# A Shen attention plus RWKV channel mix kernel: ranks of the planner passed back from the matmuls, mix-weight rows loaded by DMA, weight loads held by a wait

## The chip, the cores, the metric

The kernel runs on one core of one Trainium2 chip. The metric is the device time of one execution in microseconds (us), as a median over runs. The profile describes one of these executions; its span runs from the first to the last instruction, and the device time is about 1.8 us longer than the span. Engine names: PE is TensorE (matmuls), DVE is VectorE, ACT is ScalarE, POOL is GpSimd, SP is SyncE, which here issues loads and stores.

## The reference

Linear attention with both softmaxes, then a channel mix over its output. Shapes: q, k, v are 8 batches x 8 heads x 576 positions x 64; `w_k` is 512x1024, `w_v` 1024x512, `w_r` 512x512; everything arrives and leaves in fp32.

```python
q_s = softmax(q, axis=-1); k_s = softmax(k, axis=2)          # written out in the original
kv  = einsum('bhsd,bhse->bhde', k_s, v)
x   = einsum('bhsd,bhde->bhse', q_s, kv)                     # then (B, S, H*D)

x_prev = x shifted by one position, zero first
xk = mu_k * x + (1.0 - mu_k) * x_prev
xr = mu_r * x + (1.0 - mu_r) * x_prev
k  = np.maximum(xk @ w_k, 0.0)
v  = k * k @ w_v
r  = 1.0 / (1.0 + np.exp(-(xr @ w_r)))
return r * v
```

## The kernel before

The program is laid out by a planner written in Python. Each operation is added with its engine, how long it occupies the engine (`occ`), when its result is there (`lat`), a rank (`key`), the operations it depends on, and the buffers (`Slot`) that it takes and gives back. A list scheduler then fixes the order in which each engine's instructions are written. On the chip every engine works through its own list in that order, and semaphores make it wait where data or a buffer is not ready (in the run `g_held` below, ACT stands still for 3.22 us for a load, though the copy that comes after it in the list is ready).

```python
    def order(self):
        ...
                for op in ops:
                    if any(d.end is None for d in op.deps): continue
                    t = max([now] + [d.end + HOP for d in op.deps])
                    ...                                   # and until its buffers are free
                    rank = (max(t, now + 0.03), op.key)   # what starts first; ties by key
                    if ready is None or rank < ready[0]:
                        ready = (rank, t, op)
```

The keys of this kernel are written by hand (batch number times 200, and so on).

The work comes in two parts. *Attention* runs per batch and pair of heads (16 times): exponentials and casts on ACT, sums, scaling and mixing on DVE, and transposes and small matmuls on PE. The *main part* runs in ten units of 512 or 256 positions: the k product (line 593), ReLU on ACT (578), square on DVE (582), the r product (624), tanh on ACT (629), the v product (634), gating on DVE (640), store.

For batch 0 the mix with the shifted sequence is folded into the small matmuls of attention, which needs `mu` and `1 - mu` laid out as block masks. These rows are built by small fp32 matmuls:

```python
    def emit_mu_rows(m):
        for s in range(2):
            for ct in range(CT):
                for u in range(2):
                    to = mu_rows(m, s)[:, 128 * ct + 64 * u:128 * ct + 64 * u + 64]
                    nc.tensor.matmul(to, lhsT=pick[:, 4 * m + ct, u, :],          # line 305
                                     rhs=mu_sb[:, 64 * u:64 * u + 64], start=True,
                                     stop=(s == 0), skip_group_check=True)
                    if s == 1:
                        nc.tensor.matmul(to, lhsT=flip[:, u, :], rhs=ones[:],      # line 309
                                         start=False, stop=True, skip_group_check=True)
```

The loads of the weights and of batches 1 to 7 go out on POOL and are made to depend on one load of batch 0, `gate = [first[GATE]]` with `GATE = 7`: the second half of v of batch 0's first group. In the planner that orders their issue; nothing on the chip waits for the landing.

The softmax here doesn't subtract the row's maximum and nothing guards it: scores larger than these inputs give would overflow.

## Time and profile before

| | before |
|---|---|
| device time | 251.0 us (250.11 to 251.21) |
| span of the profiled run | 249.3 us |
| first k matmul of the main part | 38.9 us |
| last matmul ends | 244.4 us |

The page of the kernel before. The first line is busy time with the share of the span and the number of instructions; the rows below cut the span into 40 slices of 6.2 us, and each digit is the busy share in tenths. PEclk is the granted TensorE clock, also in tenths.

```profile
PE 220.9 (89%) x1377; PEld 120.0 (48%) x1377; DVE 164.7 (66%) x371; ACT 150.1 (60%) x228; POOL 39.2 (16%) x64
...
PE   0899889999478999989989998899999999999992
...
DVE  4920153588997998898999999998944233252331
...
PEclk9999999999959999999999999999999999999999
```

TensorE looks full from the second slice on. The chain of waits of the same kernel, which follows the work that ended last back through what released it, says what this early work is. Columns: start, duration, what.

```profile
2.11 5.05 DMA mu_sb<-in_moe_mu_r_dram
...
7.53 3.51 PE bank_c L305 x16
...
18.94 3.60 PE bank_d L305 x16
...
29.40 0.60 ACT mu_mask L316
...
32.20 1.12 PE bank_b L419 x9
...
38.89 0.86 PE bank_c L593 x4
```

From 7.5 to 29.4 us the chain is almost all small fp32 matmuls of lines 305 and 309. The first matmul of line 593, the k product, comes at 38.89. Up to there TensorE is busy, but not with the main part.

Two windows of the kernel before, the weakest later ones. Columns: the window and its length, then busy us (and instruction count) of PE, weight loads, DVE, ACT and POOL, then granted clock, DMA share, GB/s.

```profile
60.00:70.00 10.00, 5.56 (x76) 3.55 (x75) 9.84 (x23) 9.97 (x12) 5.54 (x8) 0.94 1.03 402
70.00:80.00 10.00, 9.14 (x62) 4.20 (x59) 8.58 (x19) 7.15 (x11) 2.24 (x4) 0.71 1.02 389
```

At 60 to 70 us TensorE waits while DVE and ACT are full; the clock then falls to 0.71 on average.

### The profile page before, as it was taken

How to read it: one execution, taken by the hardware profiler on the slowest of the kernel's cores; microseconds unless marked ns; L12 is line 12 of the kernel's file. 1: busy time of each engine (PE TensorE's matmuls, PEld its weight loads, DVE VectorE, ACT ScalarE, POOL GpSimd, SP SyncE). 2: the span in 40 equal slices, each digit the busy share in tenths (PEclk: the TensorE clock that was granted, in tenths of full speed). 3: DMA queues.
4: the chain of work that ended last, by engine and by line, in shares of the span. 5: the costliest groups of instructions: out<-in, count | busy, mean ns of one | idle time of the engine just before them, and what ended most of it. 6: DMA issues, size and time to landing. Idle time of an engine off the chain costs nothing.

```text
span 249.3 us, 3772 instructions
## 1 busy us (share of the span) xinstructions
PE 220.9 (89%) x1377; PEld 120.0 (48%) x1377; DVE 164.7 (66%) x371; ACT 150.1 (60%) x228; POOL 39.2 (16%) x64
## 2 busy tenths in 40 slices
PE   0899889999478999989989998899999999999992
PEld 0899854345234444344444456444444444444550
DVE  4920153588997998898999999998944233252331
ACT  4410255699968988998689885566235144244150
POOL 7323460043531133312000000000000000000000
PEclk9999999999959999999999999999999999999999
DMA  6999999059999679976510132120240330431413
GB/s 237 274 260 206 393 392 362 9 110 363 412 393 393 192 230 325 339 238 175 144 45 0 42 84 46 41 47 0 51 111 10 84 85 0 101 70 24 103 45 84
DMA packets 16402, 40.62 MB, mean 163 GB/s; under 512 B 2296, under 2 KB 4864, under 8 KB 16384
## 3 DMA queue, kind: packets, MB, share of 16 engines
q0 software_dynamic: 8896, 27.40, 34.8%
q1 hardware_dynamic: 7200, 12.39, 18.5%
q10 hardware_dynamic: 288, 0.59, 0.7%
q8 instruction: 11, 0.18, 0.3%
q14 instruction: 7, 0.06, 0.1%
HBM read 33.56 MB, written 9.44 MB: 172 GB/s over the span
## 4 chain that ended last, share of the span: by engine, by line
PE 63%; DVE 16%; ACT 12%; issue 4%; DMA 2%; POOL 0%; DVEq 0%; ACTq 0%; POOLq 0%
PE bank_c L593 11%; PE bank_c L634 10%; PE bank_d L634 9%; PE bank_d L593 9%; PE bank_d L624 6%; PE bank_c L624 4%; PE bank_a L309 3%; PE bank_a L305 3%; DVE qs_a L397 2%; DMA mu_sb<-in_moe_mu_r_dram 2%; PE bank_b L419 2%; ACT rel_b L578 2%; DVE ot_c L640 2%; PE bank_d L305 1%; PE bank_c L305 1%
## 5 line engine op out<-in xcount | busy, mean ns | idle before, releaser
L593 PEld LDWEIGHTS <-wk_bf 128*128 128x128 bf16 x320 | 30.6, 99 | 36.2 <-issue 9.0
L593 PE MATMUL bank_c<-xk,wk_bf 128*128 128x512 bf16 (+1 forms) x176 | 39.2, 357 | 0.7 <-ACT rel_b L578 0.3
L593 PE MATMUL bank_d<-xk,wk_bf 128*128 128x512 bf16 (+1 forms) x144 | 34.7, 372 | 3.0 <-DVE ot_a L640 0.7
L624 PEld LDWEIGHTS <-xr 128*128 128x128 bf16 x144 | 13.9, 97 | 18.6 <-issue 2.9
L624 PE MATMUL bank_d<-wr_bf,xr 128*128 128x512 bf16 x84 | 21.5, 378 | 0.9 <-ACT rel_c L578 0.6
L634 PEld LDWEIGHTS <-k_a 128*128 128x128 bf16 x144 | 13.5, 98 | 16.8 <-issue 1.8
L634 PEld LDWEIGHTS <-k_b 128*128 128x128 bf16 x144 | 13.6, 97 | 16.0 <-issue 1.2
L634 PE MATMUL bank_d<-wv_bf,k_a 128*128 128x512 bf16 x72 | 18.3, 379 | 0.9 <-ACT th_b L629 0.6
L634 PE MATMUL bank_d<-wv_bf,k_b 128*128 128x512 bf16 x72 | 18.5, 379 | 0.7 <-ACT th_a L629 0.6
L634 PE MATMUL bank_c<-wv_bf,k_b 128*128 128x512 bf16 x72 | 18.0, 379 | 0.2
L634 PE MATMUL bank_c<-wv_bf,k_a 128*128 128x512 bf16 x72 | 18.0, 379 | 0.0
L629 ACT ACTIVATE th_a<-bank_d 128x512 f32<-128x512 f32 x15 | 9.0, 602 | 12.8 <-PE bank_d L624 8.2
L624 PE MATMUL bank_c<-wr_bf,xr 128*128 128x512 bf16 x60 | 15.4, 379 | 0.3 <-ACT rel_c L578 0.3
L578 ACT ACTIVATE rel_b<-bank_c 128x512 bf16<-128x512 f32 (+1 forms) x16 | 8.9, 557 | 8.3 <-PE bank_c L593 8.3
L578 ACT ACTIVATE rel_a<-bank_c 128x512 bf16<-128x512 f32 (+1 forms) x16 | 8.5, 532 | 6.9 <-PE bank_c L593 6.4
L578 ACT ACTIVATE rel_c<-bank_d 128x512 bf16<-128x512 f32 (+1 forms) x14 | 7.6, 540 | 7.4 <-PE bank_d L593 4.2
L582 DVE TENSOR_TENSOR k_a<-rel_b 128x512 bf16<-128x512 bf16 (+1 forms) x14 | 5.7, 404 | 7.3 <-ACT rel_b L578 6.9
L316 ACT ACTIVATE mu_mask<-bank_a 128x512 f32<-128x512 f32 x2 | 1.2, 602 | 15.3 <-PE bank_a L309 15.3
L582 DVE TENSOR_TENSOR k_a<-rel_a 128x512 bf16<-128x512 bf16 (+1 forms) x13 | 5.1, 393 | 8.0 <-ACT rel_a L578 7.8
L629 ACT ACTIVATE th_b<-bank_c 128x512 f32<-128x512 f32 x12 | 7.2, 601 | 4.9 <-PE bank_c L624 2.0
L305 PE MATMUL bank_a<-mu_sb,pick 8*128 8x64 f32 x32 | 10.1, 416 | 0.0
L309 PE MATMUL bank_a<-ones,flip 1*128 1x64 f32 x32 | 10.1, 416 | 0.0
(214 smaller groups left out, 436.7 us busy)
## 6 DMA issues: line engine op xcount, KB each, us to landing
out_dram<-ot_a SPq DMA_DIRECT2D x24, 128.0 KB, 2.4
out_dram<-ot_b SPq DMA_DIRECT2D x24, 128.0 KB, 2.4
out_dram<-ot_c SPq DMA_DIRECT2D x24, 128.0 KB, 2.4
raw_a<-in_q_dram POOLq DMA_DIRECT2D x3, 576.0 KB, 6.2
raw_b<-in_k_dram POOLq DMA_DIRECT2D x3, 576.0 KB, 7.0
raw_c<-in_v_dram POOLq DMA_DIRECT2D x3, 576.0 KB, 7.7
raw_d<-in_q_dram POOLq DMA_DIRECT2D x3, 576.0 KB, 8.4
raw_e<-in_k_dram POOLq DMA_DIRECT2D x3, 576.0 KB, 9.0
```

The lines of the kernel that those rows point to most:

```text
L305: nc.tensor.matmul(to, lhsT=pick[:, 4 * m + ct, u, :], rhs=mu_sb[:, 64 * u:64 * u + 64], start=True, stop=(s == 0), skip_group_check=True)
L309: nc.tensor.matmul(to, lhsT=flip[:, u, :], rhs=ones[:], start=False, stop=True, skip_group_check=True)
L316: nc.scalar.mul(out=mu_mask[:, m, s, :, :].rearrange("p c e -> p (c e)"), in_=mu_rows(m, s), mul=(1.0, -1.0)[s])
L397: nc.vector.tensor_tensor(out=to[:, :, u, :], in0=eqs[eq.index][:, :, u, :], in1=by[:, :, :, None].to_broadcast((128, J, u.stop - u.start, ...
L419: nc.tensor.transpose(out=transposed()[:, j, :], in_=qss[qs.index][:, j, :], identity=ident[:])
L578: nc.scalar.activation(out=rels[rel.index][:, 0:n], in_=bank(kf)[:, 0:n], func=ACT.Relu, scale=HALF_ROOT)
L582: nc.vector.tensor_tensor(out=k2s[k2.index][:, fc, 0:n], in0=rels[rel.index][:, 0:n], in1=rels[rel.index][:, 0:n], op=ALU.mult)
L593: nc.tensor.matmul(bank(kf)[:, 0:n], lhsT=wk_bf[:, ct, fc * 128:(fc + 1) * 128], rhs=xs[0][:, ct, c0:c0 + n], start=(ct == 0), stop=(ct == ...
L624: nc.tensor.matmul(bank(rps), lhsT=xs[1][:, ct, c:c + 128], rhs=wr_bf[:, ct, :], start=(ct == 0), stop=(ct == CT - 1))
L629: nc.scalar.activation(out=ths[th.index][:], in_=bank(rps), func=ACT.Tanh, scale=0.5)
L634: nc.tensor.matmul(bank(vps), lhsT=k2s[k2.index][:, ft, 128 * m:128 * m + 128], rhs=wv_bf[:, ft, :], start=(ft == 0), stop=(ft == FT - 1))
L640: nc.vector.scalar_tensor_tensor(out=ots[ot.index][:], in0=ths[th.index][:], scalar=1.0, in1=bank(vps), op0=ALU.add, op1=ALU.mult)
```

## The change

Its intent: start the main part earlier, by taking the fp32 row matmuls off TensorE and by letting batch 0's data land before the weights, and let attention come when the matmuls need it, not according to hand-written ranks. There are three pieces.

1. **Ranks are due times.** The main part gets a clock (`MAIN`, `PACE`); every other operation starts with the key `LATE`, and `set_due` passes the due time back through the dependencies. `LOOK` lets the scheduler prefer a more urgent operation that is ready up to 0.3 us later, and `AHEAD` asks for the mixed rows 2 to 5 us early. With it go corrected durations, casts of v on ACT only, four `wp` buffers in place of three, and a second unit in the form in which the first half of the channels is multiplied before the second is there (`early`).
2. **The mu rows by DMA**: four loads that repeat a row over 64 partitions, and eight DVE operations that write the masks.
3. **The wait**: the first w_k load is made to wait for the landing of the gate's load.

```diff
+LOOK = {"PE": 0.03, "ACT": 0.3, "DVE": 0.2, "POOL": 0.03, "SP": 0.03}
+AHEAD = (0.0, 2.0, 5.0)
+MAIN = 18.5
+PACE = 1.23
 GATE = 7
-CASTS = (("ACT", "DVE"), ("ACT", "DVE"))
+CASTS = (("ACT", "ACT"), ("ACT", "ACT"))
...
+    def set_due(self):
+        after = {}
+        for op in self.ops:
+            for d in op.deps:
+                after.setdefault(d, []).append(op)
...                                    # walk the graph, users first
+                    for o in after.get(op, ()):
+                        op.key = min(op.key, o.key - op.lat - HOP - SPARE)
+                    op.key -= op.early
...
-                    rank = (max(t, now + 0.03), op.key)
+                    rank = (max(t, now + LOOK[engine]), op.key)
...
-    def emit_mu_rows(m):               # 48 fp32 matmuls (96 in the profile), and four ACT copies
+    def emit_mu_rows_load(m):
+        src = (moe_mu_k, moe_mu_r)[m]
+        for u in range(2):
+            ap = bass.AP(tensor=src.tensor, offset=src.offset + 256 * u, ap=[[0, 64], [1, 256]])
+            nc.scalar.dma_start(
+                out=mu_rows[64 * u:64 * u + 64, m, :, :].rearrange("p c e -> p (c e)"), in_=ap)
+    def emit_mu_mask(m):
+        for u in range(2):
+            r = slice(64 * u, 64 * u + 64)
+            nc.vector.tensor_copy(out=mu_mask[r, m, 0, :, r], in_=mu_rows[r, m, :, :])
+            nc.vector.tensor_scalar(out=mu_mask[r, m, 1, :, r], in0=mu_rows[r, m, :, :],
+                                    scalar1=-1.0, scalar2=1.0, op0=ALU.mult, op1=ALU.add)
...
+    def emit_wk(h):
+        for u in range(2):
+            ld = weight_part(wk_bf, moe_w_k, F, u, 512 * h, 512 * h + 512)
+            if h == u == 0:
+                tc.add_manual_dep(ld.ins, gate[0].made.ins.name, sync)
...
-        base = 1000 + 200 * b
-        step = base + (0 if b == 0 else 60 * g)
+        step = LATE
...
-        early = half == 0 and c0 == 0
+        early = half == 0 and c0 < 1024
```

More of the change, by code (lines that the diff above doesn't have):

```diff
@@ L18 @@
 HOP = 0.05
+LATE = 1e6
+SPARE = 0.0
+LOOK = {"PE": 0.03, "ACT": 0.3, "DVE": 0.2, "POOL": 0.03, "SP": 0.03}
+AHEAD = (0.0, 2.0, 5.0)
+MAIN = 18.5
+PACE = 1.23
 DMA_RATE = 395.0
-DMA_LEAD = 1.5
+DMA_LEAD = 1.9
 DMA_TAIL = 0.6
@@ L26 @@
 ORDER = (0, 1, 2)
+SOON = {(1, 0, 0): 1.2, (1, 0, 1): 1.4, (1, 0, 2): 1.5}
 GATE = 7
+MU_KEY = (0.5, 1.9, LATE, LATE)
 ON_PE = (0,)
-CASTS = (("ACT", "DVE"), ("ACT", "DVE"))
+CASTS = (("ACT", "ACT"), ("ACT", "ACT"))
 EVAC = ((("ACT", "DVE"), ("ACT", "ACT")), (("ACT", "DVE"), ("ACT", "ACT")))
@@ L48, in __init__ @@
         self.start = self.end = None
+        self.early = 0.0
         for slot in gives:
@@ L87, in warm @@
         return busy > 2.0
+    def set_due(self):
[3 more added lines that the diff above has]
+                after.setdefault(d, []).append(op)
+        seen = set()
+        for root in self.ops:
+            stack = [(root, False)]
+            while stack:
+                op, closed = stack.pop()
+                if closed:
+                    for o in after.get(op, ()):
+                        op.key = min(op.key, o.key - op.lat - HOP - SPARE)
+                    op.key -= op.early
+                elif op not in seen:
+                    seen.add(op)
+                    stack.append((op, True))
+                    stack += [(o, False) for o in after.get(op, ())]
     def order(self):
+        self.set_due()
         free = {}
@@ L168 @@
     assert B % 4 == 0
-    pools = {"raw": 12, "eq": 3, "ek": 2, "vv": 2, "stat": 4, "qs": 2, "qt": 3, "w": 3, "wp": 3,
+    pools = {"raw": 12, "eq": 3, "ek": 2, "vv": 2, "stat": 4, "qs": 2, "qt": 3, "w": 3, "wp": 4,
              "rz": 3, "xb": 2, "xd": 2, "xm": 3, "k2": 2, "rel": 3, "th": 2, "ot": 3, "mm": 4,
@@ L216 @@
     identf = const.tile([8, 8], F32, name="identf")
-    pick = const.tile([8, 8, 2, 128], F32, name="pick")
-    flip = const.tile([1, 2, 128], F32, name="flip")
-    ones = const.tile([1, 64], F32, name="ones")
+    mu_rows = const.tile([128, 2, CT, 64], F32, name="mu_rows")
     mu_mask = const.tile([128, 2, 2, CT, 128], F32, name="mu_mask")
@@ L236, in emit @@
                          ap=[[J * D, 128], [4 * S * D, u.stop - u.start], [1, J * D]])
-            queues[engine].dma_start(out=raws[slot.index][:, u, :], in_=ap)
+            return queues[engine].dma_start(out=raws[slot.index][:, u, :], in_=ap)
         ops = [plan.add(e, 0.71 if e == "POOL" else 0.45, 0.5, key + 0.1 * n,
@@ L266, in emit_consts, with emit_mask_zeros @@
         nc.vector.tensor_copy(out=identf[:], in_=ident[0:8, 0:8])
-        nc.vector.memset(pick[:].rearrange("p r u c -> p (r u c)"), 0.0)
-        nc.vector.memset(flip[:].rearrange("p u c -> p (u c)"), 0.0)
-        nc.vector.memset(ones[:], 1.0)
-        for u in range(2):
-            r = slice(64 * u, 64 * u + 64)
-            nc.vector.tensor_copy(out=pick[:, :, u, r],
-                                  in_=identf[:, :, None].to_broadcast((8, 8, 64)))
-            nc.vector.memset(flip[:, u, r], -1.0)
         for t in vvs:
             nc.vector.memset(t[:, :, 128:130], 1.0)
+    def emit_mask_zeros():
+        nc.gpsimd.memset(mu_mask[:].rearrange("p m s c e -> p (m s c e)"), 0.0)
     def emit_late_consts():
@@ L287 @@
     identity = plan.add("POOL", 0.6, 0.8, -8, emit_identity)
-    consts = plan.add("DVE", 2.4, 2.5, -9, emit_consts, [identity])
-    late_consts = plan.add("DVE", 0.6, 0.7, 1008, emit_late_consts)
-    mu_slot = [Slot("mm") for _ in range(3)] + [Slot("att")]
+    consts = plan.add("DVE", 0.5, 0.6, -9, emit_consts, [identity])
+    late_consts = plan.add("DVE", 0.6, 0.7, LATE, emit_late_consts)
+    mask_zeros = plan.add("POOL", 2.2, 2.3, -7, emit_mask_zeros)
+    mu_slot = Slot("mm")
     def emit_mu():
-        nc.tensor.transpose(out=bank(mu_slot[0])[:, 0:8], in_=mu_sb[:], identity=identf[:])
@@ L296, in mu_rows @@
-    def mu_rows(m, s):
-        return bank(mu_slot[1 + m]) if s == 0 else bank(mu_slot[3])[:, m, :]
-    def emit_mu_rows(m):
-        for s in range(2):
-            for ct in range(CT):
-                for u in range(2):
-                    to = mu_rows(m, s)[:, 128 * ct + 64 * u:128 * ct + 64 * u + 64]
-                    nc.tensor.matmul(to, lhsT=pick[:, 4 * m + ct, u, :],
-                                     rhs=mu_sb[:, 64 * u:64 * u + 64], start=True,
-                                     stop=(s == 0), skip_group_check=True)
-                    if s == 1:
-                        nc.tensor.matmul(to, lhsT=flip[:, u, :], rhs=ones[:],
-                                         start=False, stop=True, skip_group_check=True)
@@ L312, in emit_mu_copy @@
-    def emit_mu_copy():
-        nc.vector.tensor_copy(out=mu[:], in_=bank(mu_slot[0])[:, 0:8])
-    def emit_mu_mask(m, s):
-        nc.scalar.mul(out=mu_mask[:, m, s, :, :].rearrange("p c e -> p (c e)"),
-                      in_=mu_rows(m, s), mul=(1.0, -1.0)[s])
-    mu_t = plan.add("PE", 0.2, 0.4, -500, emit_mu, [mu_load, consts], mu_slot[0:1])
-    mu_done = plan.add("DVE", 0.08, 0.17, 1100, emit_mu_copy, [mu_t], gives=mu_slot[0:1])
+        nc.tensor.transpose(out=bank(mu_slot)[:, 0:8], in_=mu_sb[:], identity=identf[:])
@@ new lines, in emit_mu_copy @@
+    def emit_mu_copy():
+        nc.vector.tensor_copy(out=mu[:], in_=bank(mu_slot)[:, 0:8])
+    def emit_mu_rows_load(m):
[10 more added lines that the diff above has]
+                                    scalar1=-1.0, scalar2=1.0, op0=ALU.mult, op1=ALU.add)
@@ L321 @@
+    mu_t = plan.add("PE", 0.2, 0.4, -500, emit_mu, [mu_load, consts], [mu_slot])
+    mu_done = plan.add("DVE", 0.08, 0.17, LATE, emit_mu_copy, [mu_t], gives=[mu_slot])
     mu_masked = []
     for m in range(2):
-        o = plan.add("PE", 2.0, 2.2, -450 + 500 * m, lambda m=m: emit_mu_rows(m), [mu_t],
-                     [mu_slot[1 + m]] + mu_slot[3:] * (m == 0))
-        mu_masked.append([plan.add("ACT", 0.48, 0.6, 1000.5 + 130 * m,
-                                   lambda m=m, s=s: emit_mu_mask(m, s), [o],
-                                   gives=[mu_slot[1 + m] if s == 0 else mu_slot[3]])
-                          for s in range(2)])
+        o = plan.add("ACT", 0.9, 0.9, MU_KEY[m], lambda m=m: emit_mu_rows_load(m), size=131.0)
+        mu_masked.append(plan.add("DVE", 1.0, 1.1, MU_KEY[2 + m], lambda m=m: emit_mu_mask(m),
+                                  [o, mask_zeros]))
@@ L332, in weight_part @@
                      ap=[[n, 64], [D * n, CT], [1, c1 - c0]])
-        nc.gpsimd.dma_start(out=dst[64 * u:64 * u + 64, :, c0:c1], in_=ap)
+        return nc.gpsimd.dma_start(out=dst[64 * u:64 * u + 64, :, c0:c1], in_=ap)
     gate = [first[GATE]]
+    sync = mybir.DependencyInfo(mybir.DependencyClass.Sync, mybir.DependencyReason.DATA)
+    def emit_wk(h):
[3 more added lines that the diff above has]
+                tc.add_manual_dep(ld.ins, gate[0].made.ins.name, sync)
     wk_done, wv_done = [], []
@@ L338 @@
         wk_done.append(plan.add(
-            "POOL", 1.25, 1.25, h, lambda h=h: [
-                weight_part(wk_bf, moe_w_k, F, u, 512 * h, 512 * h + 512) for u in range(2)],
-            gate, size=1048.0))
+            "POOL", 1.25, 1.25, h, lambda h=h: emit_wk(h), gate, size=1048.0))
     wr_done = plan.add("POOL", 1.25, 1.25, 2, lambda: [
@@ L356 @@
             for n, i in enumerate(ORDER):
-                load(["POOL"] * (2 if b == 1 else 1), b, g, i, 100 * b + 10 * g + n, gate)
+                load(["POOL"] * (2 if b == 1 else 1), b, g, i,
+                     SOON.get((b, g, i), 100 * b + 10 * g + n), gate)
     mixed = {}
@@ L426, in flat @@
             return bank(slot).rearrange("p a c -> p (a c)")
-        pe_key = -400 + step / 1e4
+        pe_key = LATE
         us = PARTS[len(lq)]
@@ L450, in attention @@
             else:
-                castv.append(plan.add("DVE", 0.1 + 0.6 * f, 0.2 + 0.6 * f, step + 2,
+                castv.append(plan.add("DVE", 0.07 + 1.2 * f, 0.15 + 1.2 * f, step + 2,
                                       lambda u=u: cast_v(nc.vector.tensor_copy, u),
                                       [lv[n], consts], [vv] if one else [], [sv]))
-        tr = plan.add("PE", 0.61, 0.78, pe_key, transpose_q, scaled + [identity], [qtp], [qs])
+        tr = plan.add("PE", 0.5, 0.667, pe_key, transpose_q, scaled + [identity], [qtp], [qs])
         qcopy = plan.add("ACT", 1.0, 1.12, step + 3, copy_qt, [tr], [qt], [qtp])
-        kvm = plan.add("PE", 0.72, 0.9, pe_key, kv, expk + castv, [kvp], [ek, vv])
+        kvm = plan.add("PE", 0.63, 0.7, pe_key, kv, expk + castv, [kvp], [ek, vv])
         zdone = plan.add("DVE", 0.066, 0.15, step + 2, recz, [kvm], [rz])
@@ L481, in attention @@
                 wp = Slot("wp")
-                late = base + 130 + g if m else step + 3
+                late = LATE
                 mixed[b, g, m] = []
@@ L486, in attention @@
                                   lambda wp=wp, m=m, hf=hf, s=s: weights_of(wp, m, hf, s),
-                                  [zdone, mu_masked[m][s]], [wp] if hf == s == 0 else [],
+                                  [zdone, mu_masked[m]], [wp] if hf == s == 0 else [],
                                   [kvp, rz])
@@ L490, in attention @@
                     xp = Slot("att")
-                    o = plan.add("PE", 0.52, 0.69, pe_key + (300 if m else 0),
+                    o = plan.add("PE", 0.49, 0.66, pe_key,
                                  lambda wp=wp, xp=xp, hf=hf: x_mixed(wp, xp, hf), [qcopy] + o,
@@ L538, in mix @@
                                     op=ALU.add)
-        wdone = plan.add("DVE", 0.5, 0.6, step + 4, weights, [zdone, late_consts], [w],
+        wdone = plan.add("DVE", 0.61, 0.59, step + 4, weights, [zdone, late_consts], [w],
                          [kvp, rz])
@@ L543, in attention @@
         for hf in range(2):
-            o = plan.add("PE", 0.26, 0.43, pe_key, lambda hf=hf: x(hf),
+            o = plan.add("PE", 0.245, 0.41, pe_key, lambda hf=hf: x(hf),
                          [qcopy, wdone], [xps[hf]], [qt, w])
@@ L550, in attention @@
         for m in range(2):
-            late = base + 130 + g if m else step + 7
+            late = LATE
             s = [plan.add("DVE", 0.28, 0.366, late, lambda m=m, hf=hf: scale_x(m, hf),
@@ L560 @@
             attention(b, g)
-    clock = 0.0
+    clock = MAIN
     def unit(half, c0, n):
@@ L584, in square @@
                                         in1=rels[rel.index][:, 0:n], op=ALU.mult)
-            r = plan.add("ACT", 0.05 + n / 1200, 0.18 + n / 1200, clock, relu, [mm], [rel],
+            r = plan.add("ACT", 0.05 + n / 1200, 0.18 + n / 1200, clock + 1.5, relu, [mm], [rel],
                          [kf])
-            squares.append(plan.add("DVE", 0.06 + n / 1920, 0.15 + n / 1920, clock, square,
+            squares.append(plan.add("DVE", 0.06 + n / 1920, 0.15 + n / 1920, clock + 3.0, square,
                                     [r], [] if squares else [k2], [rel]))
@@ L612, in unit @@
                         [kfs[i]] if cts[0] == 0 else [])
-                    clock += per * len(cts)
+                    clock += PACE * per * len(cts)
             for i in range(step):
@@ L656, in unit @@
             rdone.append(r)
-            t = plan.add("ACT", 0.476, 0.6, clock, tanh, [r], [th], [rps])
-            clock += 0.864
+            t = plan.add("ACT", 0.476, 0.6, clock + 1.5, tanh, [r], [th], [rps])
+            clock += PACE * 0.864
             o = plan.add("PE", 0.864, 1.03, clock, lambda v=v_part: v(range(0, 4)),
                          squares[0:4] + wv_done[0:1], [vps])
-            clock += 0.864
+            clock += PACE * 0.864
             o = plan.add("PE", 0.864, 1.03, clock, lambda v=v_part: v(range(4, 8)),
                          squares[4:8] + [o] + wv_done[1:2], [], [k2])
-            clock += 0.864
-            o = plan.add("DVE", 0.593, 0.683, clock, gated, [o, t], [ot], [vps, th])
+            clock += PACE * 0.864
+            o = plan.add("DVE", 0.593, 0.683, clock + 1.5, gated, [o, t], [ot], [vps, th])
             plan.add("SP", 0.9, 0.9, 100 + clock, store, [o], [], [ot], size=262.0)
@@ L680 @@
                         o.deps += rdone
+    for (b, g, m), made in mixed.items():
+        for o in made:
+            o.early = AHEAD[min(b, 2)]
     for op in plan.order():
-        op.emit()
+        op.made = op.emit()
 _INS = ['q', 'k', 'v', 'moe_mu_k', 'moe_mu_r', 'moe_w_k', 'moe_w_v', 'moe_w_r']
```

## The prediction

> **What bounds it now (profile span 249.3 us; measured time 1.8 us more).** Three stages, by the timeline and the chain of waits:
>
> 1. To 38.9 us no matmul of the main part (k, r, v products) runs. The chain of waits reads: wait for the mu_r load (to 7.2), then fp32 matmuls building mu rows (lines 305, 309: 7.4-17.7 and 18.9-29.3[...]), then the rest of batch 0's exp/cast, transposes, kv product and mixing at the cold rate (9 transposes 1.07 us; 0.61 later). TensorE is "busy" there, but on 21 us of setup that holds up the kv product. Batch 0's last v half lands only near 17.3: weights share the DMA engines (the last v takes 10.1 us to land, the first q 3.8). The Trainium skill, "DMA: Bandwidth & Descriptors", section "Queues, rings and completion order", says each DMA engine goes round-robin between queue rows; the rising landing times agree.
> 2. 38.9-182 us: attention of batches 1-7 beside the main part. DVE is 92% busy in 82-182, TensorE 93%; at 57-73 the chain is almost all DVE, TensorE is busy 5.6 of 10 us in 60-70, and the granted clock is 0.71 in 70-80.
> 3. 182-234: TensorE 100% busy, DVE 35%. Attention had run far ahead.
>
> **What changes.**
> - Out: 21 us of fp32 matmuls, about 3 us of DVE constants, four 0.6 us ACT mask copies. In: four 64 KB DMAs (ACT queue), eight DVE ops (0.3 us each, an estimate from 128x256 shapes), one POOL memset of about 2 us in POOL's free time.
> - Weights wait for v of batch 0, first group. 3.5 MB of batch 0 at the 390 GB/s seen in 30-45 us then lands near 11.5 instead of 17; both w_k halves near 17; batch 1 group 0 near 21, w_r near 24, w_v by 30, batch 1 group 1 near 34.5.
> - Batch 0 then is bound by DVE/ACT: about 11 us of each from 4.6-5 us, plus kv, mixing and copies. First main matmul near 19.5.
> - Attention comes when due, so DVE and ACT serve ReLU, square and gating sooner.
>
> **Critical path after.** Main matmuls 159 us at the 17.66 us per unit seen at 199-217; attention of batches 1-7 is 14 x 1.75 = 24.5, batch 0's xr mixing 2: 185.5 us of TensorE. Before: 38.9 + 185.5 + 4.8 tail = 229; 20 us were stalls. After: 19.5 + 185.5 + 4.8 = 210 of span. I add 6 us of stalls: 2-3 waiting for batch 1 group 1 near 40, the rest where DVE is tight (per batch 13.7 us attention + 6.3 main = 20 of TensorE's 22.7) until about 100 us. The halved clock of 70-80 should go (3 us; in the 20). Span 215-216, time **217 us, range 209-228**. Faster by over 2%: 0.97; within 2%: 0.02; slower: 0.01. So 19.4 us from the start, 14 from stalls.
>
> **What would show it.** First k matmul at 18-22 us; no fp32 row matmuls; last batch 0 load before 13; TensorE under 9 of 10 only near 38-45 us; no slice of granted clock under 0.9 after 45; DVE busy spread to about 200 us.
>
> **What would make it wrong.** The order comes from modelled times: where ACT or a DMA lags them, in-order queues stall TensorE (225-230). Attention just in time leaves little reserve: late mixes at units 1 to 3 cost 5-10 us. Nearly no stalls: 210-212.

## More of the kernel before

The accumulators of the main part are four PSUM banks. They are declared as the halves of two tiles of two banks each:

```python
    banks = [psum.tile([128, 2, 512], F32, name=f"bank_{x}") for x in "abcd"]
    ps = {"mm": [banks[2 + i // 2][:, i % 2, :] for i in range(4)],
          "att": [t[:, :, :] for t in banks[0:2]], "early": [t[:, :, :] for t in banks[2:4]]}
```

So `bank_c` and `bank_d` in the profile are each two accumulators. Attention uses `bank_a` and `bank_b`; the kv product of batch 0 alone uses `bank_c` and `bank_d` whole.

## The result and the profile after

| | before | after |
|---|---|---|
| device time | 251.0 us | 230.44 us (230.39 to 231.45, 4 runs) |
| ratio | | 0.920, interval 0.916 to 0.923 |
| span of the profiled run | 249.3 us | 228.7 us |
| first k matmul | 38.9 us | 22.6 us |
| last matmul ends | 244.4 us | 224.1 us |

A ratio here and below is the mean time of one kernel's fast runs over that of the kernel before in the same rounds, so it is not quite the ratio of the two medians. Every kernel below gave correct results.

The page of the kernel after, the lines that answer to those of before:

```profile
PE 196.1 (86%) x1281; PEld 98.1 (43%) x1281; DVE 164.9 (72%) x368; ACT 152.3 (67%) x228; POOL 41.6 (18%) x65
...
PE   0076999967899878998979999999999999999881
...
DVE  1774855898899959989787989699578538832521
...
PEclk9999999999999999999999999999999999999999
```

96 matmul records and 25 us of TensorE's busy time are gone, the clock keeps its 9 everywhere, and DVE stays in use to about 200 us instead of falling off at 180 us. But TensorE still has 7s and 8s as late as 120 us (slices of 5.7 us), and in several of those slices DVE is not full either. The windows of the kernel after say it in numbers:

```profile
50.00:60.00 10.00, 7.28 (x62) 3.61 (x62) 8.93 (x17) 8.63 (x12) 4.61 (x7) 1.00 1.04 399
...
80.00:90.00 10.00, 7.61 (x41) 3.48 (x40) 7.26 (x17) 8.59 (x12) 2.17 (x3) 1.00 0.68 203
...
110.00:120.00 10.00, 8.29 (x47) 4.04 (x46) 7.68 (x14) 3.09 (x5) 0.72 (x1) 1.00 0.56 139
```

At 110 to 120 us no engine is full: TensorE 8.29, DVE 7.68, ACT 3.09 of 10. That is not a shortage of any engine. They wait for one another.

The timeline of the kernel after, at the start. SPq is SP issuing; the number in brackets is idle time of the engine before it and what released it.

```profile
0.74 0.39 SPq L267 DMA_DIRECT2D raw_d<-in_v_dram  x1
...
4.66 2.51 POOL L351 DMA_DIRECT2D wk_bf<-in_moe_w_k_dram  x4
...
9.21 0.80 SPq L267 DMA_DIRECT2D raw_f<-in_v_dram  x2
...
22.63 1.44 PE L617 MATMUL bank_c<-xk,wk_bf 128*128 128x512 bf16 x4
...
26.49 1.02 PE L617 MATMUL bank_d<-xk,wk_bf 128*128 128x512 bf16 x4
```

The gate's own load, the v half into raw_d, is the very first thing that SP issues, at 0.74 us (it landed at 4.3), and the weights go out at 4.66, with no wait noted, while the last v of batch 0 is issued only at 9.21. The wait is void: it waits for a load that `set_due` pulled to the front, because the gate's due time is passed back from w_k through the very dependency that was to hold w_k.

The same sum that the prediction made can be filled in with what was measured. 185.5 us is the prediction's estimate of TensorE work from the first k matmul on; the stalls are what remains.

| | before | predicted | after |
|---|---|---|---|
| start to first k matmul | 38.9 | 19.5 | 22.6 |
| TensorE work (estimate) | 185.5 | 185.5 | 185.5 |
| tail after the last matmul | 4.8 | 4.8 | 4.6 |
| stalls (the rest) | 20 | 6 | 16.0 |
| span | 249.3 | 215.8 | 228.7 |

The start missed by 3 us and the stalls by 10. Two theories followed.

- **A**: the void wait. The weights push back batch 0's data (its last half landed at 18.8 us, where 11.5 to 13 had been predicted), the start is late, and everything after it lags.
- **C**: the shared tiles. A read of one half of `bank_c` or `bank_d` waits for matmuls into the other half, in both kernels alike; the change does not touch it.

The texts below use such letters. B and D are the rivals of A and C; E, which comes later, is that the planner's landing times are not those of the chip. In the text of `b_mu`, "theory A" is another one, which is written out there.

### The profile page after: what moved, and what is told of

It is laid out like the page before. It is cut to its first block, busy times and chain, and to the rows that moved or that the text cites. A ratio compares the mean times of both kernels' runs of the same rounds, so it can differ in the third digit from the quotient of the medians.

```text
span 228.7 us, 3591 instructions
## 1 busy us (share of the span) xinstructions
PE 196.1 (86%) x1281; PEld 98.1 (43%) x1281; DVE 164.9 (72%) x368; ACT 152.3 (67%) x228; POOL 41.6 (18%) x65
## 3 DMA queue, kind: packets, MB, share of 16 engines
q1 hardware_dynamic: 7200, 12.39, 20.1%
## 5 line engine op out<-in xcount | busy, mean ns | idle before, releaser
L617 PE MATMUL bank_d<-xk,wk_bf 128*128 128x512 bf16 (+1 forms) x160 | 37.1, 357 | 3.5 <-DVE ot_c L664 1.2
L658 PEld LDWEIGHTS <-k_a 128*128 128x128 bf16 x144 | 13.5, 97 | 18.9 <-issue 3.0
L658 PE MATMUL bank_c<-wv_bf,k_a 128*128 128x512 bf16 x80 | 20.2, 379 | 1.3 <-ACT th_b L653 1.0
L648 PE MATMUL bank_c<-wr_bf,xr 128*128 128x512 bf16 x72 | 18.5, 379 | 0.8 <-ACT rel_c L602 0.6
L648 PE MATMUL bank_d<-wr_bf,xr 128*128 128x512 bf16 x72 | 18.5, 379 | 0.5 <-ACT th_b L653 0.5
L653 ACT ACTIVATE th_a<-bank_c 128x512 f32<-128x512 f32 x10 | 6.0, 598 | 7.3 <-PE bank_c L648 3.4
L653 ACT ACTIVATE th_a<-bank_d 128x512 f32<-128x512 f32 x8 | 4.8, 599 | 6.4 <-PE bank_d L648 5.7
L602 ACT ACTIVATE rel_a<-bank_d 128x512 bf16<-128x512 f32 (+1 forms) x13 | 7.4, 570 | 1.8 <-PE bank_d L617 1.6
L443 PE MATMUL bank_a<-ident,qs_a 128*128 128x128 bf16 x72 | 5.8, 230 | 2.8 <-DVE qs_a L421 2.8
L447 ACT COPY qt_a<-bank_a 128x1152 bf16<-128x1152 bf16 x5 | 5.6, 1117 | 3.7 <-PE bank_a L443 3.7
L653 ACT ACTIVATE th_b<-bank_c 128x512 f32<-128x512 f32 x8 | 4.8, 598 | 4.8 <-PE bank_c L648 4.5
```

What stands on the lines that cost most here:

```text
L443: nc.tensor.transpose(out=transposed()[:, j, :], in_=qss[qs.index][:, j, :], identity=ident[:])
L447: nc.scalar.copy(out=qts[qt.index][:], in_=transposed()[:, 0:J, :])
L602: nc.scalar.activation(out=rels[rel.index][:, 0:n], in_=bank(kf)[:, 0:n], func=ACT.Relu, scale=HALF_ROOT)
L617: nc.tensor.matmul(bank(kf)[:, 0:n], lhsT=wk_bf[:, ct, fc * 128:(fc + 1) * 128], rhs=xs[0][:, ct, c0:c0 + n], start=(ct == 0), stop=(ct == ...
L648: nc.tensor.matmul(bank(rps), lhsT=xs[1][:, ct, c:c + 128], rhs=wr_bf[:, ct, :], start=(ct == 0), stop=(ct == CT - 1))
L653: nc.scalar.activation(out=ths[th.index][:], in_=bank(rps), func=ACT.Tanh, scale=0.5)
```

## The experiments

### The wait made real, taken away, and moved to the last load

`g_held` keeps the gate's own rank, so that the wait means what it was meant to:

```diff
-                        op.key = min(op.key, o.key - op.lat - HOP - SPARE)
+                        if not op.pinned:
+                            op.key = min(op.key, o.key - op.lat - HOP - SPARE)
...
     gate = [first[GATE]]
+    gate[0].pinned = True
```

> The changed kernel, with the load that the weights wait for kept at its own place in the queue (its due time is not passed back through the wait). Theory A (the wait was void, because that load was pulled to the front of its queue and landed at about 4.5 us; this is why the start came late): the first w_k issue moves from 4.7 to 10-11 us, the last half of batch 0's v lands near 14 instead of 19, the first run of k matmuls starts near 21 instead of 26.5, time 225 to 227. Rival B (the start is not what was lost; later weights or the DVE and ACT queues take it back): time within 1 us of the changed kernel's 230.4.

Measured: 229.77 us (228.71 to 231.0), ratio 0.916 with interval 0.912 to 0.920, which overlaps that of the change. The mechanism did what it should: w_k was issued at 11.71 us, released by the landing of raw_d; the last v half of batch 0 landed at 14.3 us in place of 18.8; the first k matmul ran at 18.97. The Trainium skill, "DMA: Bandwidth & Descriptors", section "Queues, rings and completion order", says that each DMA engine goes round-robin between the queue rows it has work for; 14.3 without the weights beside it against 18.8 with them agrees. (Even so it is not the 11.5 of the prediction: SP issued the k load before it, raw_e, only at 7.62 us, against 4.79 in the kernel before. The last section says why.) But the gain did not last. The timeline of `g_held`:

```profile
18.97 1.04 PE L620 MATMUL bank_c<-xk,wk_bf 128*128 128x512 bf16 x4
...
22.30 0.68 ACT L402 ACTIVATE eq_c<-raw_g 128x576 bf16<-128x576 f32 x1 [3.22 <-DMA raw_g<-in_q_dram]
22.89 0.62 ACT L504 CAST xr<-bank_b 128x576 bf16<-128x576 f32 x1
...
23.56 0.65 PE L499 MATMUL bank_b<-qt_b,wp_c 128*128 128x512 bf16 x5 [2.58 <-ACT xr L504]
...
26.03 1.91 PE L620 MATMUL bank_c<-xk,wk_bf 128*128 128x512 bf16 x4
```

The planner had put an exponential of batch 1 (raw_g) ahead of batch 0's copy into xr, in the belief that its data would be there. ACT runs in order: it stood 3.22 us for the load, then did the copy for which TensorE had been waiting 2.58 us. After that the clock was halved. Two of the 1-us windows of `g_held`:

```profile
21.00:22.00 1.00, 0.00 (x0) 0.00 (x0) 0.91 (x2) 0.00 (x0) 0.28 (x2) 1.00 1.06 431
...
25.00:26.00 1.00, 1.00 (x3) 0.30 (x2) 1.00 (x3) 0.96 (x3) 0.43 (x2) 0.50 1.19 205
```

Four k matmuls that took 1.04 us at 18.97 took 1.91 at 26.03. The Trainium skill, "TensorE: Matmul & The Clock Gate", section "Part 1: The HAM clock gate", lists a full and a half clock, and says that it falls to half after at least one idle window of about 3.4 us; the half clock agrees, but the gap here was only 2.58 us. By the first ReLU (27.98 us, against 28.41 in the changed kernel) 3.7 us of earlier start had become 0.4. The time is what rival B had forecast. As the cause of the missing 13 us, theory A falls.

`g_none` takes the wait out altogether (the manual dependency becomes `pass`).

> The changed kernel without the wait on the weights at all. Theory A: the wait held nothing back, so the first w_k issue stays at 4.7 us and the time within 0.5 us of 230.4. Rival B (the wait does keep the weights behind some of batch 0): first w_k issue earlier by 1 us or more and time up by 1 us or more.

Measured: 228.78 and 232.2 us in fast runs, two more runs at 232.3 (slow), ratio 0.918 (0.910 to 0.927). (Slow means here over 1.5% above the fastest run; between 232.2 and 232.3 that says little.) The time is inconclusive, and the profile fell into a slow run. What it does settle is the issue of w_k: 4.67 us without the wait, 4.66 with it. So the wait held back nothing.

`g_last` is `g_held` with `GATE = 11`, the last load of batch 0.

> As the kept-place version, but the weights wait for the very last half load of batch 0. Theory A: batch 0 lands near 13, w_k not before about 19-20; the k matmuls start near 21 and the time is between 225 and 229. Rival B (weights become the limit): above 230.

Measured: 229.77 and 231.48 us in fast runs, 233.77 and 235.24 in slow ones, ratio 0.919 (0.914 to 0.924). w_k was issued at 14.60, and the steady run of k matmuls began at 23.3 us. w_k went out 5 us earlier than expected, and the two fast runs lie on either side of the 230 of rival B: there is neither a gain nor a clear loss.

### The mu rows alone

`b_mu` is the kernel before with only piece 2 of the change, with its own ranks and no wait.

```diff
 # on the kernel before
+MU_KEY = (0.5, 1.9, 1000.5, 1130.5)
-    def emit_mu_rows(m): ...
+    def emit_mu_rows_load(m): ...       # as in the change
+    def emit_mu_mask(m): ...            # as in the change
```

> The kernel before, with its own orders, and the mu rows by DMA alone (no wait, no new orders). If the start was most of the gain (theory A: the fp32 matmuls held the kv product of batch 0 by about 12-14 us): 235 to 238, first k matmul near 25. If the new orders made half of the gain or more (rival): 240 or above. If the new orders made nothing or cost time: 231 or below.

Measured: 236.18 us (235.72 to 236.63), ratio 0.941 (0.939 to 0.944), first k matmul at 25.1 us. About 15 us of the change's 20.6 are the mu rows; due times, wait and the rest bring the last 5.7.

### One tile for each bank

`split` is the changed kernel with each of the four accumulators as a tile of its own. Nothing else moves but one detail: batch 0's two reciprocals become four small ones on DVE. The planner sees the same slots; in the built programs the lists of PE, ACT, POOL and SP are the same instruction by instruction, and the same four physical banks (4 to 7) are used.

```diff
-    banks = [psum.tile([128, 2, 512], F32, name=f"bank_{x}") for x in "abcd"]
-    ps = {"mm": [banks[2 + i // 2][:, i % 2, :] for i in range(4)],
-          "att": [t[:, :, :] for t in banks[0:2]], "early": [t[:, :, :] for t in banks[2:4]]}
+    banks = [psum.tile([128, 2, 512], F32, name=f"bank_{x}") for x in "ab"]
+    mms = [psum.tile([128, 512], F32, name=f"mm_{x}") for x in "abcd"]
+    ps = {"mm": [t[:, :] for t in mms], "att": [t[:, :, :] for t in banks],
+          "early": [[t[:, :] for t in mms[2 * i:2 * i + 2]] for i in range(2)]}
...                                     # batch 0's kv product takes two tiles,
...                                     # and each reciprocal becomes two small ones
```

> The changed kernel, its instructions in the same order on every engine, but each of the four PSUM banks of the main part is a tile of its own instead of half of a two-bank tile. Theory C (the order is sound and its reserve thin; a ReLU, tanh or gating read of one half waits for matmuls into the other half, 55 of 152 such reads in the changed program, and each such wait sets the whole fixed order back by up to 1 us): time 220 to 225, with the stalls at 50-60, 80-90 and 110-120 us halved. Rival D (TensorE loses there because DVE and ACT have too little time): within 1.5 us of 230.4.

Measured: 216.3 us (215.05 to 217.02), ratio 0.860 (0.856 to 0.864), span 213.5. That is 14.1 us below the changed kernel for one declaration, and it is below the 220 to 225 that theory C had forecast. It is also where the prediction had put the change itself (217 us, span 215 to 216), but in part by luck: `split` starts 3.4 us later than the prediction said and has less in stalls, and the two nearly cancel. The same place in both kernels shows how. The timeline of the kernel after:

```profile
77.38 1.89 PE L617 MATMUL bank_d<-xk,wk_bf 128*128 128x512 bf16 x8 [0.77 <-ACT rel_b L602]
...
79.30 0.60 ACT L602 ACTIVATE rel_c<-bank_d 128x512 bf16<-128x512 f32 x1 [1.49 <-PE bank_d L617]
79.80 1.14 ACT L406 CAST vv_a<-raw_d 128x1152 bf16<-128x1152 f32 x1
...
79.97 1.03 PE L617 MATMUL bank_d<-xk,wk_bf 128*128 128x512 bf16 x4
...
81.03 0.60 ACT L602 ACTIVATE rel_a<-bank_d 128x512 bf16<-128x512 f32 x1
...
81.68 1.02 PE L617 MATMUL bank_d<-xk,wk_bf 128*128 128x512 bf16 x4 [0.69 <-ACT rel_a L602]
```

The eight matmuls from 77.38 to 79.27 are two groups of four, one for each half of `bank_d`. The first half was complete at about 78.4. Its ReLU, rel_c, ran only at 79.30, right after the second group, with ACT idle for 1.49 us before it. The cast of 1.14 us that stands next in ACT's list then ran until 80.94. The next ReLU, rel_a, came only at 81.03: its own half had been complete at 79.27, but it too waited for the next group into the other half, the one at 79.97, which ended at 81.00. For rel_a TensorE stood still for 0.69 us at 81. The built programs say the same: by the count of TensorE's semaphore rel_c waits for 440 and rel_a for 448 here, and for 436 and 440 in `split`. The timeline of `split`, the same instructions in the same order:

```profile
74.38 1.02 PE L627 MATMUL mm_d<-xk,wk_bf 128*128 128x512 bf16 x4
75.24 1.03 PE L627 MATMUL mm_c<-xk,wk_bf 128*128 128x512 bf16 x4
...
75.44 0.60 ACT L612 ACTIVATE rel_c<-mm_d 128x512 bf16<-128x512 f32 x1
75.93 1.14 ACT L411 CAST vv_a<-raw_d 128x1152 bf16<-128x1152 f32 x1
76.98 0.60 ACT L612 ACTIVATE rel_a<-mm_c 128x512 bf16<-128x512 f32 x1
```

Here rel_c starts 0.04 us after its own four matmuls end, while the next four write the other bank. The cast fits in behind it, and no wait is noted. The Trainium skill, "PSUM — Partial Sum Buffer", section "PSUM bank collisions raise a hardware error", says that pairs of engines on different banks run clean; this agrees, as `split` was correct in all its runs. So the wait did not come from the banks: it goes with the tile that the kernel declares.

The windows of `split`, to be held against the three of the kernel after:

```profile
50.00:60.00 10.00, 8.84 (x69) 4.45 (x70) 9.93 (x18) 9.98 (x15) 4.33 (x6) 1.00 1.04 398
...
80.00:90.00 10.00, 9.90 (x56) 4.91 (x57) 9.79 (x19) 8.73 (x13) 2.87 (x4) 1.00 0.98 322
...
110.00:120.00 10.00, 9.95 (x98) 6.79 (x98) 8.68 (x23) 8.43 (x17) 0.00 (x0) 1.00 0.32 93
```

From 60 us on TensorE is full. Put into the same sum, `split` is 22.9 (first k matmul) + 185.5 + 4.6 = 213.0 of a span of 213.5: the stalls are almost gone. Not quite, as the sum makes it seem: the trace of `split` still has two waits of TensorE in this stretch, 1.42 us for a cast of v at 50.2 and 0.75 us for a ReLU at 53.8, so that the estimate of TensorE work is about 2 us too high.

The lag behind the plan tells the same. The planner's own forecast for each ReLU is subtracted from its start on the chip:

| forecast of the ReLU, us | 22.8 | 48.2 | 72.1 | 93.4 | 115.2 | 138.4 | 161.0 | 183.3 |
|---|---|---|---|---|---|---|---|---|
| lag in the changed kernel, us | 5.6 | 6.6 | 10.7 | 12.7 | 16.4 | 16.8 | 18.2 | 18.9 |
| lag in `split`, us | 5.6 | 6.0 | 6.0 | 6.0 | 6.2 | 6.4 | 6.4 | 6.6 |

Both start 5.6 us late. With the shared tiles another 13 us come bit by bit over the main part, with the tiles split only 1 us. The false waits were then counted in the built programs: for each of the 152 reads of an accumulator by ReLU, tanh or gating, it was compared which matmul its semaphore value waits for with the last matmul that wrote its own bank. In the kernel before 56 wait longer than they need, in the changed one 55, in `split` 12. A recount shows what the 12 are: reads without a wait of their own, because their engine had already waited for a later matmul. Counted without such reads, it is 55 before, 48 in the changed kernel, and none in `split`. The count also leaves out the opposite direction, which comes with the same declaration: TensorE, about to write one half, waits for a read of the other. The recount finds 93 such waits before, 106 in the changed kernel, and none in `split`. How the lost time divides between the two directions is not shown.

### The same on other kernels, and by degrees

`split_held` is `split` with the wait made real as in `g_held`.

> The same with the weights truly held behind batch 0 (as in the kept-place version). If the hold gains nothing because ACT's queue has batch 1's exp, which now lands later, ahead of batch 0's copies (theory E): within 1 us of the split version, with ACT waiting about 3 us for batch 1's q near 19-22 us. If the hold was hidden only by the shared tiles: 3 us or more below the split version.

Measured: 215.55 us (215.18 to 216.47), ratio 0.858 (0.855 to 0.862). The difference of 0.75 us to `split` lies within the scatter, and ACT waits 3.7 us for batch 1's q, as theory E had it.

`b_mu_split` is `b_mu` with the declaration of `split`, `before_split` the kernel before with it.

> The kernel before, own orders, with mu rows by DMA and the four banks as tiles of their own. Theory C: the shared tiles cost the old orders too (56 of 152 reads wait too long in the program before): 226 to 231 against 236.2. Rival: within 1.5 us of 236.2.

> The kernel before, untouched but for the four banks as tiles of their own. Theory C: the 20 us of stalls that the prediction laid to the orders were largely these waits: 238 to 243. Rival (they were the orders' doing): 248 or above.

Measured: `b_mu_split` 226.4 us (225.37 to 227.16), ratio 0.901; `before_split` 238.65 us (238.02 to 239.43), ratio 0.950. The split is worth 12.7 us on the kernel before, 9.8 on `b_mu` and 14.1 on the changed kernel; only 1 false wait is left in each of the two, and the waits were in the kernel before all along. With tiles split the due times and the rest of the bundle are worth 226.4 - 216.3 = 10.1 us; with shared tiles 5.7.

`half` splits only the second pair. `merge4` goes the other way: all four accumulators are quarters of one tile.

```diff
 # half: two accumulators share a tile, two do not
+    banks = [psum.tile([128, 2, 512], F32, name=f"bank_{x}") for x in "abc"]
+    mms = [psum.tile([128, 512], F32, name=f"mm_{x}") for x in "cd"]
 # merge4
+    four = psum.tile([128, 4, 512], F32, name="four")
+    ps = {"mm": [four[:, i, :] for i in range(4)], ...
```

> The changed kernel, same orders; only the second pair of banks split into tiles of their own, the first pair still one tile. 31 of 152 reads wait too long (55 in the changed kernel, 12 in the split one). Theory C: between the two, 221 to 226. Rival (something else in the split version made it fast): at 216 or at 230.

> The suspected cost raised: the changed kernel, same orders and same banks, but all four banks of the main part are one tile; 135 of 152 reads now wait for matmuls into other banks. Theory C: above 240. Rival: within 3 us of 230.4.

Measured: `half` 222.21 us (221.37 to 223.84), ratio 0.885; `merge4` 324.2 us (323.24 to 333.16, the highest of them slow), ratio 1.288. With the counts of false waits the four kernels of the same order line up: 12 and 216.3 us, 31 and 222.2, 55 and 230.4, 135 and 324.2. The dose moves the time in one direction, though not in proportion: the first three lie at about 0.33 us for each of these waits, and `merge4` far above. (Without the reads that have no wait of their own it is 0, 22, 48 and 126; the waits of the opposite direction are 0, 54, 106 and 136.) `half` and `merge4` have the same extra reciprocals as `split`, so these are not what made `split` fast.

`split_noearly` undoes one small part in `split`: only the first unit is multiplied in two halves of the channels, as in the kernel before.

> The split version with one small part of the change undone: only the first unit, not the first two, takes its k products in two halves over the contraction. If that part matters: 2 us or more above 216.3; if not: within 1.5 us.

Measured: 216.72 us (215.41 to 217.77), ratio 0.860. This part of the change does nothing measurable.

### A plan that knows when loads land

`told` is `split_held` with a planner that is given the landing times measured in `g_held` for batches 0 and 1, the mu rows and the weights, in place of its own forecast.

```diff
+LAND = {(0, 0, 0, 0): 4.47, ..., ("mu", 0): 7.6, ("mu", 1): 10.64, ("w", 0): 17.9, ...}
...
+                dma_free = max(dma_free, op.land - DMA_TAIL)
```

> Split and held, and the plan that fixes the order is given the landing times of batch 0, batch 1 and the weights as the held run measured them. Theory E (order fixed with landing times that the DMA does not keep): ACT no longer waits 3 us for batch 1's q; the first run of k matmuls is unbroken from about 20-21 us at the full clock; 3 to 5 us below the split version. Rival: within 1.5 us of the split version, since later stages (DMA or DVE near 40-80 us) take it back.

Measured: 214.66 us (212.99 to 215.18), ratio 0.853 (0.849 to 0.857), the fastest of all the kernels here, though only 1.6 us below `split` and 0.9 below `split_held`, whose plan alone differs; the ranges touch in both cases. That is not the gain of 3 to 5 us that theory E had forecast. ACT's longest wait for batch 1's q fell from 3.22 to 0.7 us, and the k matmuls ran from 20.1 us. Most of this earlier start was lost again. The wait list of `told` for TensorE, with total, times and longest in us, and its window of 40 to 50 us:

```profile
PE mm_a L645 <- DVE xk L588: 2.9, 2, 2.1
PE mm_c L676 <- DMA wr_bf<-in_moe_w_r_dram: 1.7, 1, 1.7
```

```profile
40.00:50.00 10.00, 6.77 (x53) 3.10 (x52) 9.36 (x22) 9.73 (x13) 5.12 (x8) 1.00 1.02 388
```

TensorE, started sooner, ran into the mixing of batch 1 on a nearly full DVE and into the load of w_r; after the longest of these waits, 2.14 us, its clock was 0.50 from 51 to 54 us. The loads and DVE's attention work set the pace there. What the remaining start would give with loads in a better order was not tried.

## Why the prediction was wrong

**The step that failed is "14 from stalls"**, with its reason "Attention comes when due, so DVE and ACT serve ReLU, square and gating sooner". By the sum, stalls fell from 20 to 16 us, not to 6. The prediction took the 20 us of before for the fault of the ranks and of a tight DVE. More than half of them, 12.7 us by `before_split`, came with the shared tiles: ReLU, tanh and gating wait for matmuls into the other half of their own tile, and TensorE waits for reads of the other half. No order of the planner can see that: it treats the four banks as separate slots. With the tiles split in the changed kernel, the stalls of the same sum are 0.5 us (at least 2 by the trace), and the time is 216.3 us.

It was there to be read before. In the program tanh reads the r product (line 624) and never the v product (line 634). The wait list of the kernel before for ACT has these lines:

```profile
ACT th_a L629 <- PE bank_d L624: 8.2, 4, 2.1
...
ACT th_a L629 <- PE bank_d L634: 3.7, 5, 1.1
ACT th_a L629 <- PE bank_c L634: 2.2, 2, 1.8
...
ACT th_b L629 <- PE bank_c L634: 1.4, 2, 0.7
```

The first is as it should be. The other three, 7.3 us in sum, are tanh waiting for matmuls whose result it does not touch. In the kernel after there are still three such lines (line 658 is the v product there):

```profile
ACT th_a L653 <- PE bank_c L658: 1.6, 2, 1.0
ACT th_a L653 <- PE bank_d L658: 0.6, 1, 0.6
ACT th_b L653 <- PE bank_c L658: 0.3, 1, 0.3
```

In the same lists of `split`, `b_mu_split` and `before_split` tanh waits for the v product nowhere. Not all of this idle time is on the critical path; what is on it is told by the 14.1 us of `split`.

Point by point:

- **"Weights wait for v of batch 0, first group"**: wrong. The gate's load was issued first and the wait was void (w_k at 4.66 us with it, 4.67 without). Batch 0's last v half landed at 18.8 us, where batch 0 was to land near 11.5. The first k matmul came at 22.6 instead of 19.5. But this was not what was missing: with the wait made real the first k matmul came at 18.97, and the time fell by 0.7 us, within the scatter.
- **"19.4 us from the start"**: 16.3, and in the right place. The mu rows by DMA alone gave 15 us.
- **TensorE work of 185.5 us**: about right; by the waits left in `split`, about 2 us too high.
- **No fp32 row matmuls, no slice of granted clock under 0.9 after 45 us**: right.
- **"TensorE under 9 of 10 only near 38-45 us"**: wrong; 7.28 in 50 to 60, 7.61 in 80 to 90, 8.29 in 110 to 120. In `split` it holds from 60 us on.
- **"DVE busy spread to about 200 us"**: right (9.07 of 10 us in 190 to 200).
- **Named among the risks**: that in-order queues stall TensorE where "ACT or a DMA lags them" (225 to 230 us). The time, 230.44, came out just above that, and the 3.22 us on ACT in `g_held` is such a stall. But the lag that grew through the main part came from the tile waits.

What stays open: which piece of the bundle in the ranks (due times, look-ahead, lead, casts on ACT, the fourth `wp` buffer, durations) brings its 5.7 to 10.1 us. Only the second `early` unit was tried by itself, and it brings nothing.

## What to carry to other kernels

Before blaming an order for stalls, read in the wait list what each engine is said to wait for and check that the instruction really reads it: a consumer that waits for a producer of something else points to buffers that share a tile. Declare accumulators that live and die apart as separate tiles, because in these programs views of one tile were bound together by its waits however well the planner ordered them. And when due times are passed back through dependencies, see that a wait's own anchor is not pulled forward by it.

## What the Trainium skill lacked or had wrong

- "PSUM — Partial Sum Buffer" speaks of collisions of engines in one bank, and not of waits that a kernel picks up when two banks are declared as one tile: here 55 of 152 reads waited too long, and 14.1 of 230.4 us went with the shared tiles; with four banks in one tile it was 135 reads and 324.2 us.
- "TensorE: Matmul & The Clock Gate", section "Part 1: The HAM clock gate", gives at least one idle window of about 3.4 us before the clock falls to half, and not how much work such a window may still hold. In `g_held` the clock was 0.50 in 25 to 28 us after a gap of 2.58 us in TensorE's work, in `told` 0.50 in 51 to 54 us after 2.14 us, and in the kernel before 0.50 in 69 to 75 us after four gaps of 0.65 to 1.19 us between 63.0 and 68.1 us.
- No page was found that says what more small loads on a second queue do to the first. In `b_mu`, where the four mu-row loads on ACT's queue are the change to the loads, SP issued raw_e at 7.71 us in place of 4.79. In the built programs the loads that SP and ACT issue take eight completion semaphores in rotation, so that a load waits for the landing of the one eight before it. The traces agree: the load that raw_e has to wait for is a half of q in the kernel before (landed at 4.78 us) and a mu-row load in `b_mu` (landed at 7.69 us).
